# Five, five, three and three partitions for the low side loads, and their zeros written by GpSimd

## The chip, the cores and the metric

The kernel runs on one core of a Trainium2 chip. The metric is the device time of one execution in microseconds. Engines are called PE (TensorE), DVE (VectorE), ACT (ScalarE), POOL (GpSimd) and SP (SyncE, which issues nearly all loads); loads are carried out by 16 transfer engines that the core's queues share.

## The reference

A decode step for 8 sequences of one token each, D = 512. The input x is normalised (layer norm) and goes two ways; all inputs are bf16.

```python
xn = layernorm(x)                                   # [8, 1, 512]
q = xn @ wq                                         # 32 heads of 128
k, v = last 2048 of 8192 rows of k_cache, v_cache   # [8, 8, 2048, 128], each head used by 4 query heads
s = softmax(q k^T / sqrt(128)) v @ wo               # wq [512, 4096], wo [4096, 512]
h = sigmoid(xn @ w_gate) * (xn @ w_up)              # [8, 1792]
g = silu(h @ w_down)                                # w_down [1792, 512]
out = x + s * g
```

The windows of k and v are 67 MB of the 81 MB that are read; w_down has 1792 rows of 1 KB.

## The kernel before, in words

All large tensors are loaded by SP's queue into nine slots of SBUF. A list `todo` holds the loads in a fixed order: w_gate and w_up (two halves each), the main part of w_down, side loads and the two halves of wq mixed, then the tiles of k and v (one of 2 MB for a sequence and half its heads, k three tiles ahead of v), then wo in five pieces that get smaller (12, 8, 6, 4 and 2 of 32 row groups). `pump` takes entries from the list as long as a slot is empty, and `free` gives a slot back and calls `pump` again. A load that reuses a completion semaphore also waits for the earlier load of it; there are eight in turn.

A load into 128 partitions gives each of the 16 transfer engines eight rows. The rows of w_down are divided unevenly: 1280 rows go as ten row groups on 128 partitions (tile `wd_sb`, `want_down`), and the other 512 rows go into the tile `side` by eight small loads (`want_side`). Four of them, the low ones, bring 14 rows of w_down (14336 bytes) into each of `LOW` = 4 partitions, and four, the middle ones, 8 rows (8192 bytes) into each of `MID` = 9 partitions. The low ones lie in partitions 0 to 15, load q taking the partitions q, q + 4 and so on, the middle ones from partition 32 (`M_AT`) on. Partitions 16 to 31 are read by the matmuls of the first eight row groups (68 partitions) and hold zeros, which a DVE memset writes at line 126 before the first side load (partitions 0 to 31, the first eight row groups).

The gated layer's h is computed as [8, 1792] (lines 278 to 301), and two GpSimd copies (lines 309 and 312) put the columns that belong to the side rows in the order of its partitions into `h_side`; its gaps are zeros. PE turns h and h_side (line 320), DVE and ACT copy the result to `hT_sb`, then come the q projection (line 344) and the product with w_down (line 358).

The attention runs over the eight sequences: transposes of k (line 448, copied by DVE at line 453), scores (466), softmax, transposes of the probabilities (556), products with v (577). The last stage is 128 small matmuls with wo (line 699), then two DVE operations and the store of the output.

Of the kernel before, what the change touches and what calls it, by code (L numbers as in the profile page):

```python
# [10 lines left out]
def kernel(  # L11
# [13 lines left out]
    nc = tc.nc  # L25
    P = 128
    B, _, D = A_x.shape
# [59 lines left out]
    def pump():  # L87
        while todo and (empty or not todo[0][0]):
            slot, f = todo.pop(0)
            f(f"slot{empty.pop(0)}") if slot else f()  # L90
# [17 lines left out]

        todo.append((True, f))

    LOW, SF = 4, 14
    MID, SM = 9, 8
    SP = 4 * LOW
    M_AT = 32
    MP = 4 * MID
    MT = 10
    m0 = MT * P
    m1 = m0 + SF * SP
    assert m1 + SM * MP == F
    side = {}  # L120

    def want_side(w, first, at, count, rows, base):
        def f(tag=None):
            if tag:
                t = slots.tile([P, SF, w.shape[1]], bf16, name="side", tag=tag)
                nc.vector.memzero(t[:M_AT, :SM])  # L126
                side["t"] = t
                rows_of[("side", 0)] = (t, tag)
                for r in range(SF):
                    weights[("wd_sb", MT + r)] = t[: M_AT + MP if r < SM else SP, r]  # L130
            last = at + 4 * count
            q0.dma_start(  # L132
                out=side["t"][at + first : last : 4, :rows].rearrange(
                    "p s n -> p (s n)"
                ),
                in_=w[base : base + 4 * count * rows, :].rearrange(
                    "(p s) n -> p (s n)", s=rows
                )[first : 4 * count : 4],
            )

        todo.append((not side, f))
        side["asked"] = True

    def want_down(w):
        def f(tag):
            t = slots.tile([P, MT, w.shape[1]], bf16, name="wd_sb", tag=tag)
            q0.dma_start(
                out=t[:].rearrange("p t n -> p (t n)"),
                in_=w[: MT * P, :].rearrange("(p t) n -> p (t n)", t=MT),
            )  # L150
            rows_of[("wd_sb", 0)] = (t, tag)
            for r in range(MT):
                weights[("wd_sb", r)] = t[:, r, :]

        todo.append((True, f))

    def want_cache(tiles, cache, name, b, i):
# [14 lines left out]
    want_rows("wg_sb", B_w_gate, KT, 0, KT, 2)  # L172
    want_rows("wu_sb", B_w_up, KT, 0, KT, 2)
    want_down(B_w_down)
    sides = [
        (q, *x) for q in range(4) for x in ((0, LOW, SF, m0), (M_AT, MID, SM, m1))
    ]
    for x in sides[:2]:
        want_side(B_w_down, *x)
    for i in range(2):  # L180
        want_rows("wq_sb", A_wq, KT, 2 * i, 2 * i + 2)
        for x in sides[2 + 3 * i : 5 + 3 * i]:
            want_side(B_w_down, *x)
# [7 lines left out]
    for t0, t1 in ((0, 12), (12, 20), (20, 26), (26, 30), (30, RT)):  # L191
# [1 line left out]

    x_bf = work.tile([B, D], bf16, name="x_bf")
    q1.dma_start(out=x_bf[:], in_=A_x.flatten_outer_dims())
    pump()

    ident = consts.tile([P, P], bf16, name="ident")
    make_identity(nc, ident[:])
    ident_f = consts.tile([P, P], f32, name="ident_f")  # L200
    make_identity(nc, ident_f[:])

    perm = consts.tile([P, P], bf16, name="perm")
    nc.vector.tensor_copy(
        out=perm[:].rearrange("k (l p) -> k l p", l=G),
        in_=ident[:].rearrange("k (p l) -> k l p", l=G),
# [13 lines left out]
        out=rstd[:], in_=mv[:, 1:2], func=AF.Sqrt, bias=eps_t[:], scale=1.0  # L220
# [4 lines left out]
        out=xn_bf[:],  # L225
# [8 lines left out]
    for kt in range(KT):  # L234
        nc.tensor.transpose(
            out=xnT_ps[:, kt, :],
            in_=xn_bf[:].rearrange("b (p kt) -> b kt p", kt=KT)[:, kt, :],
# [18 lines left out]
    h_side = work.tile([B, SF, M_AT + MP], bf16, name="h_side")  # L256
# [6 lines left out]
    with nc.allow_low_precision(reason="zeros and a one"):  # L263
        nc.vector.reduce_sum(
            out=band[:], in_=ident[:].rearrange("k (q t) -> k q t", t=RT), axis=AX.X
        )
        nc.vector.reduce_sum(
            out=pick[:], in_=ident[:].rearrange("k (q t) -> k t q", t=RT), axis=AX.X
# [21 lines left out]
    h_bf = ktpool.tile([P, CU * P], bf16, name="h_bf", tag="kT")  # L290
    for k in range(F // FC):
        u_ps = ps_t.tile([B, FC], f32, name="u_ps", tag="t")
        for kt in range(KT):
# [8 lines left out]
            out=h_bf[:B, k * FC : (k + 1) * FC],  # L302
# [3 lines left out]
        )  # L306
    free(rows_of[("wu_sb", 0)])
    hT_ps = ps_m.tile([P, MT + SF, B], bf16, name="hT_ps", tag="m")
    nc.gpsimd.tensor_copy(
        out=h_side[:, :, :SP], in_=h_bf[:B, m0:m1].rearrange("b (p t) -> b t p", t=SF)  # L310
    )
    nc.gpsimd.tensor_copy(
        out=h_side[:, :SM, M_AT:],
        in_=h_bf[:B, m1:F].rearrange("b (p t) -> b t p", t=SM),
    )
    cuts = [h_bf[:B, :m0].rearrange("b (p t) -> b t p", t=MT)[:, t] for t in range(MT)]
    rows = [P] * MT + [M_AT + MP] * SM + [SP] * (SF - SM)
    cuts += [h_side[:, t, : rows[MT + t]] for t in range(SF)]
    for t, x in enumerate(cuts):
        nc.tensor.transpose(  # L320
            out=hT_ps[: rows[t], t, :], in_=x, identity=ident[:B, :B]
        )
    nc.vector.tensor_copy(out=hT_sb[:, :MT, :B], in_=hT_ps[:, :MT])
    for k, t0, t1 in ((M_AT + MP, MT, MT + SM), (SP, MT + SM, MT + SF)):
        nc.scalar.copy(out=hT_sb[:k, t0:t1, :B], in_=hT_ps[:k, t0:t1])
# [41 lines left out]
    for e in range(2):  # L367
# [3 lines left out]
        for r in range(rep):  # L371
            nc.tensor.transpose(  # L372
                out=qT_ps[:, r].rearrange("p g z -> p (g z)"),
                in_=q_bf[:, r * Dh : (r + 1) * Dh],
# [3 lines left out]
            out=qm_sb[:, :, G * e : G * (e + 1), M0 : M0 + rep].rearrange(  # L378
                "p b g r -> p r g b"
            ),  # L380
            in_=qT_ps[:, :, :, :B],
# [14 lines left out]
    for j in range(NB):  # L396
# [15 lines left out]
        out=turn_rows[:].rearrange("k (x l r) -> k x l r", x=NU, l=G),  # L412
        in_=ident[:].rearrange("k (l x r) -> k x l r", x=NU, l=G),
    )
    sel_e = consts.tile([P, 2, Hq], f32, name="sel_e")
    for e in range(2):
        nc.vector.reduce_sum(
            out=sel_e[:, e, :].rearrange("k (i h) -> k i h", i=NQ),
            in_=ident_f[:].rearrange(
                "k (i m e h) -> k e i h m", i=NQ, m=NJ // 2, e=2  # L420
            )[:, e],
# [243 lines left out]
    last = B - 1  # L665
# [47 lines left out]
    for j in range(NB):  # L713
        (q0, q1)[j % 2].dma_start(
            out=out.flatten_outer_dims()[:, j * P : (j + 1) * P],
            in_=y_bf[Z * j : Z * j + B, :],
# [31 lines left out]
```

## Time and profile before

| | us |
|---|---|
| median of 3 runs | 200.63 (200.6 to 200.64) |
| the profiled execution | 200.46 |
| its span, first to last instruction | 198.69 |
| PE busy | 159.2 (80%) |
| DVE busy | 126.7 (64%) |
| ACT busy | 40.5 (20%) |
| POOL busy | 5.7 (3%) |
| mean rate of the loads | 409 GB/s, 81.32 MB |

The profile's first part gives each engine's busy time, its second 40 equal slices of the span, the third the queues with the time of their packets as a share of all 16 transfer engines, the fourth the chain of work that ended last. The timeline and the chain in order of time give start and length in us from the span's start. In the slices the transfer engines are at 9 tenths or more in all but the first and the last two.

### The profile page before, as it was taken

How to read it: one execution, taken by the hardware profiler on the slowest of the kernel's cores; microseconds unless marked ns; L12 is line 12 of the kernel's file. 1: busy time of each engine (PE TensorE's matmuls, PEld its weight loads, DVE VectorE, ACT ScalarE, POOL GpSimd, SP SyncE). 2: the span in 40 equal slices, each digit the busy share in tenths (PEclk: the TensorE clock that was granted, in tenths of full speed). 3: DMA queues.
4: the chain of work that ended last, by engine and by line, in shares of the span. 5: the costliest groups of instructions: out<-in, count | busy, mean ns of one | idle time of the engine just before them, and what ended most of it. 6: DMA issues, size and time to landing. Idle time of an engine off the chain costs nothing.

```text
span 198.7 us, 4852 instructions
## 1 busy us (share of the span) xinstructions
PE 159.2 (80%) x2136; PEld 105.1 (53%) x2136; DVE 126.7 (64%) x259; ACT 40.5 (20%) x95; POOL 5.7 (3%) x15
## 2 busy tenths in 40 slices
PE   0695369998786998799979995999999768976752
PEld 0233125776663565556646654666777456655541
DVE  6824006999795696579667963379789657935201
ACT  3330022006206000700160016000340060071000
POOL 8002000000000000000000000000000000000000
PEclk9999559999999999999999998599999999999975
DMA  6999999999999999999999999999999999999970
GB/s 221 427 442 430 421 429 432 422 429 427 426 435 429 432 426 429 429 429 432 429 426 430 435 424 429 432 426 429 432 426 426 435 422 435 429 434 411 423 287 5
DMA packets 6540, 81.32 MB, mean 409 GB/s; under 512 B 828, under 2 KB 836, under 8 KB 1732
## 3 DMA queue, kind: packets, MB, share of 16 engines
q1 hardware_dynamic: 6472, 81.01, 96.0%
q8 instruction: 16, 0.26, 0.5%
q14 instruction: 4, 0.03, 0.0%
q10 hardware_dynamic: 48, 0.01, 0.0%
HBM read 81.01 MB, written 0.01 MB: 408 GB/s over the span
## 4 chain that ended last, share of the span: by engine, by line
DMA 69%; PE 23%; DVE 6%; issue 1%; SPq 0%
DMA v_sb<-in_A_v_cache_dram 33%; DMA k_sb<-in_A_k_cache_dram 18%; PE kT_ps L448 12%; DMA wo_sb<-in_A_wo_dram 10%; DMA wq_sb<-in_A_wq_dram 8%; PE o_ps L577 4%; PE s_ps L466 3%; DVE kT_sb L453 2%; PE m_ps L607 1%; PE pT_ps L556 1%; DVE side L126 1%; DVE pT_sb L561 1%; PE fin_ps L699 1%; SPq L132 0%; DVE stats L213 0%
## 5 line engine op out<-in xcount | busy, mean ns | idle before, releaser
L453 DVE COPY kT_sb<-kT_ps 128x1024 bf16<-128x1024 bf16 x128 | 83.8, 683 | 29.3 <-PE kT_ps L448 24.8
L448 PE MATMUL kT_ps<-perm,k_sb 128*128 128x128 bf16 x1024 | 73.9, 222 | 3.9 <-DMA k_sb<-in_A_k_cache_dram 3.7
L448 PEld LDWEIGHTS <-k_sb 128*128 128x128 bf16 x1024 | 60.0, 99 | 24.9 <-issue 16.8
L577 PE MATMUL o_ps<-v_sb,pT_sb 128*32 128x256 bf16 (+1 forms) x384 | 34.8, 315 | 9.8 <-DMA v_sb<-in_A_v_cache_dram 8.3
L466 PE MATMUL s_ps<-kT_sb,qm_sb 128*32 128x512 bf16 x256 | 26.0, 396 | 1.4 <-DVE kT_sb L453 1.1
L486 ACT ACTIVATE p_buf<-s_ps,st 32x512 bf16<-32x512 f32 x32 | 21.7, 679 | 15.7 <-DVE st L479 15.4
L577 PEld LDWEIGHTS <-pT_sb 128*32 128x32 bf16 (+1 forms) x384 | 12.8, 100 | 21.7 <-issue 18.8
L597 ACT ACTIVATE o_sb<-o_ps,fac 128x512 f32<-128x512 f32 (+1 forms) x8 | 4.6, 581 | 59.9 <-PE o_ps L577 59.9
L561 DVE COPY pT_sb<-pT_ps 128x1024 bf16<-128x1024 bf16 x16 | 10.8, 676 | 1.8 <-PE pT_ps L556 1.8
L466 PEld LDWEIGHTS <-qm_sb 128*32 128x32 bf16 x256 | 7.1, 93 | 8.3 <-issue 1.7
L556 PE MATMUL pT_ps<-turn_rows,p_buf 128*128 128x128 bf16 x128 | 10.7, 227 | 0.0
L556 PEld LDWEIGHTS <-p_buf 128*128 128x128 bf16 x128 | 9.4, 149 | 0.2 <-issue 0.2
L513 ACT ACTIVATE w_row<-w 1x128 f32<-1x128 f32 x8 | 2.5, 308 | 32.6 <-DVE w L506 32.6
L377 DVE COPY qm_sb<-qT_ps 128x128 bf16<-128x128 bf16 x2 | 1.4, 884 | 11.9 <-PE qT_ps L372 11.9
L344 PE MATMUL q_ps<-wq_sb,xnT_sb 128*32 128x512 bf16 x32 | 3.7, 617 | 5.4 <-DMA wq_sb<-in_A_wq_dram 5.4
L278 PE MATMUL g_ps<-wg_sb,xnT_sb 128*8 128x448 bf16 x16 | 6.3, 575 | 1.1 <-DMA wg_sb<-in_B_w_gate_dram 0.8
L699 PE MATMUL fin_ps<-wo_sb,oP_sb 128*32 128x128 bf16 x128 | 3.8, 274 | 2.7 <-DMA wo_sb<-in_A_wo_dram 2.3
L486 ACT ACTIVATION_READ_ACCUMULATOR p_buf<-s_ps,st 32x1 f32 x32 | 5.9, 184 | 0.0
L479 DVE TENSOR_REDUCE st<-s_ps 128x1 f32<-128x512 f32 x8 | 5.5, 683 | 0.5 <-PE s_ps L466 0.5
L301 DVE TENSOR_TENSOR h_bf<-sig,u_ps 8x448 bf16<-8x448 f32 x4 | 2.4, 608 | 4.1 <-PE u_ps L294 3.7
L344 PEld LDWEIGHTS <-xnT_sb 128*32 128x32 bf16 x32 | 1.2, 125 | 7.1 <-issue 7.1
L607 PE MATMUL m_ps<-ident_f,o_sb 128*128 128x32 f32 x32 | 5.0, 304 | 0.0
(88 smaller groups left out, 84.9 us busy)
## 6 DMA issues: line engine op xcount, KB each, us to landing
k_sb<-in_A_k_cache_dram SPq DMA_DIRECT2D x16, 2048.0 KB
v_sb<-in_A_v_cache_dram SPq DMA_DIRECT2D x16, 2048.0 KB, 30.5
wq_sb<-in_A_wq_dram SPq DMA_DIRECT2D x2, 2048.0 KB, 14.3
wg_sb<-in_B_w_gate_dram SPq DMA_DIRECT2D x2, 896.0 KB
wu_sb<-in_B_w_up_dram SPq DMA_DIRECT2D x2, 896.0 KB, 10.0
wo_sb<-in_A_wo_dram SPq DMA_DIRECT2D x1, 1536.0 KB
wd_sb<-in_B_w_down_dram SPq DMA_DIRECT2D x1, 1280.0 KB
wo_sb<-in_A_wo_dram SPq DMA_DIRECT2D x1, 1024.0 KB
```

Source lines behind the costliest of these rows:

```text
L278: nc.tensor.matmul(g_ps[:], lhsT=xnT_sb[:, kt, :B], rhs=weights[("wg_sb", kt)][:, k * FC : (k + 1) * FC], start=(kt == 0), stop=(kt == KT ...
L344: nc.tensor.matmul(q_ps[e][Z * g : Z * (g + 1), :], lhsT=xnT_sb[:, kt, :], rhs=weights[("wq_sb", kt)][:, c0 : c0 + D], start=(kt == 0), st ...
L448: nc.tensor.transpose(out=kT_ps[:, c, :], in_=k_sb[:, j * CU + h * CH + c, :], identity=perm[:],)
L453: nc.vector.tensor_copy(out=kT[(b, u)][:, h * CH : (h + 1) * CH, :], in_=kT_ps[:])
L466: nc.tensor.matmul(s_ps[b][NR * l : NR * (l + 1), :], lhsT=qm_sb[:, b, i * G + l, o : o + Z], rhs=t[:, :, PG * l : PG * (l + 1)], start=(u ...
L479: nc.vector.tensor_reduce(out=st[b][:], in_=s_ps[b][:], axis=AX.X, op=ALU.max, negate=True)
L486: nc.scalar.activation(out=p_buf[b % 2][rows, :, l, :], in_=s[rows, :].rearrange("k (c p) -> k p c", p=PG), func=AF.Exp, bias=st[b][rows, ...
L556: nc.tensor.transpose(out=pT_ps[:, c, :], in_=p_buf[b % 2][:, :, :, h * CH + c].rearrange("k p l -> k (p l)"), identity=turn_rows[:],)
L561: nc.vector.tensor_copy(out=pT[b][:, h * CH : (h + 1) * CH, :], in_=pT_ps[:])
L577: nc.tensor.matmul(o_ps[r] if b < WIDE else o_ps[r, 0:2], lhsT=pT[b][:, c, r], rhs=x, start=(c == 0), stop=(c == CU - 1), tile_position=(0 ...
L607: nc.tensor.matmul(oT_ps, lhsT=o[:, e, :], rhs=sel[:, e], start=(e == 0), stop=(e == n - 1),)
L699: nc.tensor.matmul(fin_ps[Z * j : Z * (j + 1), :], lhsT=oP_sb[:, t, :], rhs=weights[("wo_sb", t)][:, j * P : (j + 1) * P], start=(t == 0), ...
```

## The change

The four low loads take 5, 5, 3 and 3 partitions in place of 4 each; the total of 16 rows of 14 stays. Load q still takes the partitions q, q + 4 and so on, so the low part now reaches to partition 19 (`SP` = 20), and loads 0 and 1 share one run of w_down's rows, loads 2 and 3 another. Partitions 14, 15, 18 and 19 get no row, so zeros are needed there in all 14 row groups: the memset now covers partitions 0 to 31 with all row groups, 3584 words of 4 bytes each, and is GpSimd's. The call of `pump` that starts the loads stands behind the two `make_identity`, so that this memset is queued behind GpSimd's work for them. The first GpSimd copy of `h_side` becomes two, and the short row groups have 20 partitions in place of 16.

```diff
-    LOW, SF = 4, 14
+    LOW, SF = (5, 5, 3, 3), 14
     MID, SM = 9, 8
-    SP = 4 * LOW
+    SP = 4 * max(LOW)
...
-    m1 = m0 + SF * SP
+    m1 = m0 + SF * sum(LOW)
...
-    def want_side(w, first, at, count, rows, base):
+    def want_side(w, q, at, count, rows, base, of):
         def f(tag=None):
             if tag:
                 t = slots.tile([P, SF, w.shape[1]], bf16, name="side", tag=tag)
-                nc.vector.memzero(t[:M_AT, :SM])
+                nc.gpsimd.memzero(t[:M_AT])
...
-            last = at + 4 * count
             q0.dma_start(
-                out=side["t"][at + first : last : 4, :rows].rearrange(
+                out=side["t"][at + q : at + q + 4 * (count - 1) + 1 : 4, :rows].rearrange(
                     "p s n -> p (s n)"
                 ),
-                in_=w[base : base + 4 * count * rows, :].rearrange(
-                    "(p s) n -> p (s n)", s=rows
-                )[first : 4 * count : 4],
+                in_=w[base : base + of * count * rows, :].rearrange(
+                    "(p q s) n -> q p (s n)", q=of, s=rows
+                )[q % of],
             )
...
-    sides = [
-        (q, *x) for q in range(4) for x in ((0, LOW, SF, m0), (M_AT, MID, SM, m1))
-    ]
+    sides = []
+    for q in range(4):
+        sides.append((q, 0, LOW[q], SF, m0 + q // 2 * 2 * LOW[0] * SF, 2))
+        sides.append((q, M_AT, MID, SM, m1, 4))
...
-    pump()
 
     ident = consts.tile([P, P], bf16, name="ident")
     make_identity(nc, ident[:])
     ident_f = consts.tile([P, P], f32, name="ident_f")
     make_identity(nc, ident_f[:])
+    pump()
...
-    nc.gpsimd.tensor_copy(
-        out=h_side[:, :, :SP], in_=h_bf[:B, m0:m1].rearrange("b (p t) -> b t p", t=SF)
-    )
+    for h in range(2):
+        c = LOW[2 * h]
+        at = m0 + h * 2 * LOW[0] * SF
+        nc.gpsimd.tensor_copy(
+            out=h_side[:, :, : 4 * c].rearrange("b t (e q) -> b t e q", q=4)[
+                :, :, :, 2 * h : 2 * h + 2
+            ],
+            in_=h_bf[:B, at : at + 2 * c * SF].rearrange(
+                "b (e q t) -> b t e q", q=2, t=SF
+            ),
+        )
```

## The prediction

> **What bounds the kernel now.** I read the page's chain of work that ended last, then the queues, then the end of the chain in order of time, and last the single DMA packets that the trace records.
>
> The chain, by engine:
>
> ```profile
> DMA 69%; PE 23%; DVE 6%; issue 1%; SPq 0%
> ```
>
> Two thirds of the last chain is waiting for transfers. The queue rows say how full the transfer engines are:
>
> ```profile
> q1 hardware_dynamic: 6472, 81.01, 96.0%
> q8 instruction: 16, 0.26, 0.5%
> q14 instruction: 4, 0.03, 0.0%
> ```
>
> All loads are on q1, and their packets fill 96% of the span on the mean of 16 engines. What ends the kernel is the chain's tail (start, length, what):
>
> ```profile
> 174.91 19.21 DMA wo_sb<-in_A_wo_dram
> 194.12 0.04 issue
> 194.16 0.62 PE fin_ps L699 x15
> 194.78 0.02 issue
> 194.80 0.43 PE fin_ps L699 x8
> ```
>
> TensorE waits for the last pieces of wo, and the eight matmuls at 194.80 need the very last load. A load is complete when the slowest of its engines is done, so I followed the engines one by one. The packet records have no engine number, but on an engine one packet follows the other within a few ns (a 16384-byte packet every 607 ns), and every load ends with one 4-byte record for each engine it used. A 128-partition load leaves 16 of them, a nine-row side load nine, a four-row side load four. So 16 sequences can be chained, and the side packets (14336 bytes for the low rows, 8192 for the middle ones) show that the same four engines take all low rows and that these four are also among the nine. That makes three kinds of engine. End of the last wo packet, us in the span, a star for each instruction fetch (q8, 16 KB) and a plus for each of the 8 KB fetches of q14 that fell between an engine's packets:
>
> ```
> four engines with low and middle rows   192.73  192.77  193.38+  194.46++
> five engines with middle rows only      190.49  191.09  191.22+  193.26**  193.43**
> seven engines without side rows         189.54  192.08** 192.24** 192.28** 192.88** 193.04** 193.17**
> ```
>
> After the first loads the only time lost is these fetches (0.84 us for each of the two on the last engine, about 1.4 for each q8 one) and 0.5 and 1.1 us near 24 us on two of the seven. The last engine ends at 194.46, the next at 193.43: one engine alone holds the kernel for 1.03 us. Its last landing plus 0.34 is the 194.80 at which the last matmuls start.
>
> **The change part by part.** The profiled execution took 200.46 us, its span 198.69 and 1.77 around it; the median of the runs is 200.63, 0.17 more. I work in the span and take the difference to the median.
>
> *Rows moved.* Of the four low loads two get five rows and two get three. By the nesting seen above, the first three engines keep four rows each, the fourth goes from four to two, and a fifth gets two that had none. A row is one packet of 14336 bytes: its record is 535 ns, the next packet of the engine follows 531 later, and the 4-byte record takes 6, so 537 ns a row and 1.07 us for two. [...]
>
> If the late engine is the fourth, it ends at 194.46 - 1.07 = 193.39, and the last is then the 193.43 of an engine that I take to be untouched. The gain is 194.46 - 193.43 = 1.03 us. It goes through to the end if TensorE is ready: after 189.14 it has 128 small matmuls, the third last batch would be done by 191.06, the next waits for a landing at 191.53 + 0.34 and takes 0.83, the one before the last lands by 192.78 + 0.34 and needs 0.62 to 193.74, and the last eight start at 193.43 + 0.34 = 193.77. That is just enough; a loss of 0.1 is possible.
>
> *The zeros and the wait.* The call that starts the loads moves behind the identities, but SyncE's list of loads keeps its order. The VectorE memset of 1.76 us goes. A GpSimd one of 32 x 3584 words comes in behind the two identities, and SyncE's first side load now waits for it:
>
> ```profile
> 1.52 1.70 POOL masks.py:199 TENSOR_SCALAR_AFFINE_SELECT ident_f<-ident_f 128x128 f32<-128x128 f32 x1
> 3.17 0.69 POOL L253 MEMSET hT_sb<- 128x384 uint32 x1
> 3.79 0.52 POOL L255 MEMSET oP_sb<- 128x512 uint32 x1
> ```
>
> The step from oP_sb to the next start is 0.47 us for 512 words, 0.92 ns each; hT_sb's 0.62 for 384 is 1.6 each. So 3584 words take 3.3 to 5.8 us; I take 3.3, the longer tile being nearer. The select before it took 1.70 beside the VectorE memset where its bf16 twin took 0.29, so the start is 1.8 to 3.2 and the end 5.1 to 9.0. What waits behind it on SyncE:
>
> ```profile
> 2.78 0.66 SPq L147 DMA_DIRECT2D wd_sb<-in_B_w_down_dram  x1
> 3.48 1.64 SPq L132 DMA_DIRECT2D side<-in_B_w_down_dram  x2
> 5.16 0.46 SPq L101 DMA_DIRECT2D wq_sb<-in_A_wq_dram  x1
> 5.70 4.88 SPq L132 DMA_DIRECT2D side<-in_B_w_down_dram  x3
> 12.16 0.34 SPq L101 DMA_DIRECT2D wq_sb<-in_A_wq_dram  x1
> ```
>
> Two side loads, the first half of wq, three side loads. The engines finish wd between 13.93 and 14.86; until then they are fed. The first half of wq was issued 1.68 after the side load and the first packet of the kernel came 1.05 after its issue (0.74 to 1.79), so the memset may end as late as 13.93 - 2.73 = 11.2 before an engine runs dry. At 5.1 to 9.0 the cost is nothing. SyncE has caught up before the wq load at 12.16 or shortly after, and what follows that is not needed by the engines until wq's first half is done, at 18.9.
>
> GpSimd's three memsets (1.5 us in all) move back to end at 6.7 to 10.6; pick_f, at 10.69, is the first that could notice. VectorE, one memset shorter, can have the normalised x about 0.5 us earlier, which buys nothing because TensorE then waits for w_gate until 7.85. It could also be later. [...] Either way TensorE's front work has this cover:
>
> ```profile
> 20.25 1.84 PE L344 MATMUL q_ps<-wq_sb,xnT_sb 128*32 128x512 bf16 x16 [1.02 <-DMA wq_sb<-in_A_wq_dram]
> 26.50 1.90 PE L344 MATMUL q_ps<-wq_sb,xnT_sb 128*32 128x512 bf16 x16 [4.41 <-DMA wq_sb<-in_A_wq_dram]
> ```
>
> Up to 1.02 us of delay disappears before 20.25, up to 4.41 more before 26.50, while three k loads stand in the queues.
>
> *Copies and shapes.* The GpSimd copy of h_side (0.56 us, 8x224) becomes two of the same total; one fixed cost more, between 0 and another 0.56. It delays transposes that sit before the 1.02 us wait. Twenty partitions instead of sixteen in the six short tiles cost no time: the instructions have the same length along the free side.
>
> Sum: -1.03 + 0 + 0 + 0 = -1.03 us, from 200.63 to **199.60**.
>
> **The rivals.**
>
> *The late engine is another of the four (no change).* Then it still has four low rows and ends at 194.46: 200.63. The trace does not number the four. What I can see is whose fetches hold it up: between its two fetches (at 48.0 and 118.7) VectorE ran 125 instructions, and 8 KB at PE's rate of 4272 instructions to 16 fetches of 16 KB is 134, so it serves VectorE's instruction stream. The fetch at 104.6 on another of the four fits ScalarE's 63rd instruction, the one at 177.1, on an engine of the five, SyncE's 82nd. If such streams lie on neighbouring engines, the one across the border is the fifth, and VectorE's is the fourth or one further down. The late engine is also the last of the four to start, its first packet at 2.37 against 1.79 to 1.83, as one served after the others would. Blind the fourth has one chance in four; with both hints I choose 0.68. [...] Under this rival I also count that the fifth engine is one with PE fetches: 193.26 or 193.43 plus 1.07 is 194.33 or 194.50, a gain of 0.13 or a loss of 0.04. Together 0.22.
>
> *The bound is a slow transfer engine elsewhere (no change).* [...] Here 16384 bytes take 611 ns in all 16 sequences wherever no fetch falls, and the three latest engines lie in the first two kinds; I give it 0.02, inside the 0.22.
>
> *The queue runs dry (slower).* If GpSimd is held by VectorE's three memsets after 6.41 (1.66 + 0.91 + 0.91), the memset ends at 9.0 + 3.5 = 12.5 and the engines idle 1.3 us from 13.93. All 16 lose it: 201.9 without the gain above, 200.9 with it. It decides from an end of 11.2 on. Against it: both ends of the cost must be at their worst. 0.10.
>
> **How the numbers follow.** The fourth engine is the late one, with 0.68: 199.6, own range 199.4 to 199.9. No change 0.22, slower 0.10. This kernel's runs differ by 0.02%, and 0.2% (0.4 us) is about what a comparison can tell from nothing; the gain of 1.03 is 0.5%. The range must reach the no-change case, so 199.4 to 200.8; what is left out is most of the slower case.
>
> **What would show it.** In the packets after: low side loads with five, five, three and three 14336-byte packets; the sequence with the two 8 KB fetches holding two of them and ending near 193.4; the last wo matmuls at about 193.8. GpSimd's memset of side should end before 11.2 and SyncE's second wq load be issued near 12.2. If the sequence with two 8 KB fetches still holds four low packets, the identification failed; if there is a gap in all sequences after wd, the wait did.

## The result and the profile after

The changed kernel takes 199.76 us (five runs, 199.69 to 199.85) against 200.63 (five runs, 200.40 to 200.64): a ratio of 0.9959, interval 0.9945 to 0.9974, a gain of 0.87 us. Its profiled execution took 199.72 with a span of 197.9. The prediction was 199.6.

The chain that ended last, by engine, and its tail in order of time (start, length, what), of the changed kernel:

```profile
DMA 67%; PE 26%; DVE 4%; SPq 1%; issue 0%
```

```profile
174.40 18.90 DMA wo_sb<-in_A_wo_dram
193.30 0.04 issue
193.35 0.62 PE fin_ps L707 x13
193.97 0.01 issue
193.98 0.43 PE fin_ps L707 x6
```

The bound is the same, the load of wo, and the last matmuls start at 193.98 where they started at 194.80: 0.82 us, nearly the whole gain, sits in this landing. (The chain names 13 and 6 of the 16 and 8 matmuls; the trace has all of them.) Chained as in the prediction, the packets say which transfer engine is last. End of the last wo packet, us in the span; a star is a 16 KB instruction fetch on that engine (taken to be PE's, whose 4272 instructions are by far the longest stream; from one such fetch to the next it starts 262 of them on the mean), a plus an 8 KB one:

```
four low rows (first three engines)    192.69  192.74  193.38+
two low rows (fourth and fifth)        192.09+  193.29++
middle rows only (four engines)        190.40  191.12  193.57**  193.60**
no side rows (seven engines)           189.83  191.59*  192.43**  192.46**  192.48**  192.72**  192.87**
```

The low loads run on five, five, three and three engines, and the engine with the two 8 KB fetches is one of the two that now hold two low rows, which went there from four or from none. It held four before, so it is the fourth. It ends at 193.29 in place of 194.46. The next engines now set the end, two that hold middle rows only and carry PE's fetches; they ended at 193.26 and 193.43 before.

At the front, the zeros and the loads behind them. GpSimd's memset and VectorE's cast of x in the changed kernel (start, length, engine, line):

```profile
1.52 0.29 POOL masks.py:199 TENSOR_SCALAR_AFFINE_SELECT ident_f<-ident_f 128x128 f32<-128x128 f32 x1
1.75 3.07 POOL L126 MEMSET side<- 32x3584 uint32 x1
```

```profile
2.21 3.25 DVE L211 CAST x_f<-x_bf 8x512 f32<-8x512 bf16 x1 [0.65 <-DMA x_bf<-in_A_x_dram]
```

The same cast in the kernel before:

```profile
3.00 0.49 DVE L211 CAST x_f<-x_bf 8x512 f32<-8x512 bf16 x1
```

SyncE's list and TensorE's rows after the change:

```profile
4.86 1.67 SPq L131 DMA_DIRECT2D side<-in_B_w_down_dram  x2
6.57 0.46 SPq L101 DMA_DIRECT2D wq_sb<-in_A_wq_dram  x1
7.07 3.62 SPq L131 DMA_DIRECT2D side<-in_B_w_down_dram  x3
12.15 0.34 SPq L101 DMA_DIRECT2D wq_sb<-in_A_wq_dram  x1
```

```profile
20.30 1.29 PE L352 MATMUL q_ps<-wq_sb,xnT_sb 128*32 128x512 bf16 x16 [1.84 <-DMA wq_sb<-in_A_wq_dram]
26.56 1.90 PE L352 MATMUL q_ps<-wq_sb,xnT_sb 128*32 128x512 bf16 x16 [4.96 <-DMA wq_sb<-in_A_wq_dram]
```

The side loads start 1.4 us later (4.86, before 3.48), and SyncE has caught up by the second wq load at 12.15 (before 12.16). The cast of x lasts 3.25 us in place of 0.49: it starts inside the memset and ends at 5.46, 0.64 after the memset's end at 4.82. Yet TensorE reaches the q matmuls with 1.84 us to wait (before 1.02), and 4.96 in the second row.

### The profile page after: what moved, and what is told of

It is laid out like the page before. It is cut to its first block, busy times and chain, and to the rows that moved or that the text cites. A ratio compares the mean times of both kernels' runs of the same rounds, so it can differ in the third digit from the quotient of the medians.

```text
span 197.9 us, 4853 instructions
## 1 busy us (share of the span) xinstructions
PE 157.6 (80%) x2136; PEld 104.7 (53%) x2136; DVE 128.4 (65%) x258; ACT 40.5 (20%) x95; POOL 7.5 (4%) x17
## 4 chain that ended last, share of the span: by engine, by line
DMA 67%; PE 26%; DVE 4%; SPq 1%; issue 0%
DMA v_sb<-in_A_v_cache_dram 45%; PE kT_ps L456 12%; DMA wo_sb<-in_A_wo_dram 10%; DMA wq_sb<-in_A_wq_dram 7%; DMA wu_sb<-in_B_w_up_dram 5%; PE o_ps L585 4%; PE s_ps L474 3%; DVE kT_sb L461 3%; PE d_ps L366 2%; PE m_ps L615 1%; PE pT_ps L564 1%; PE q_ps L352 1%; SPq L101 1%; DVE pT_sb L569 1%; PE fin_ps L707 1%; PE qT_ps L380 0%
## 5 line engine op out<-in xcount | busy, mean ns | idle before, releaser
L585 PE MATMUL o_ps<-v_sb,pT_sb 128*32 128x256 bf16 (+1 forms) x384 | 35.9, 326 | 8.5 <-DMA v_sb<-in_A_v_cache_dram 7.0
L585 PEld LDWEIGHTS <-pT_sb 128*32 128x32 bf16 (+1 forms) x384 | 13.4, 104 | 20.6 <-issue 17.4
L352 PE MATMUL q_ps<-wq_sb,xnT_sb 128*32 128x512 bf16 x32 | 3.2, 536 | 6.8 <-DMA wq_sb<-in_A_wq_dram 6.8
L278 PE MATMUL g_ps<-wg_sb,xnT_sb 128*8 128x448 bf16 x16 | 4.5, 452 | 0.3 <-DVE xnT_sb L242 0.3
L707 PE MATMUL fin_ps<-wo_sb,oP_sb 128*32 128x128 bf16 x128 | 3.2, 252 | 1.6 <-DMA wo_sb<-in_A_wo_dram 1.1
```

The source lines that it names most:

```text
L278: nc.tensor.matmul(g_ps[:], lhsT=xnT_sb[:, kt, :B], rhs=weights[("wg_sb", kt)][:, k * FC : (k + 1) * FC], start=(kt == 0), stop=(kt == KT ...
L352: nc.tensor.matmul(q_ps[e][Z * g : Z * (g + 1), :], lhsT=xnT_sb[:, kt, :], rhs=weights[("wq_sb", kt)][:, c0 : c0 + D], start=(kt == 0), st ...
L585: nc.tensor.matmul(o_ps[r] if b < WIDE else o_ps[r, 0:2], lhsT=pT[b][:, c, r], rhs=x, start=(c == 0), stop=(c == CU - 1), tile_position=(0 ...
L707: nc.tensor.matmul(fin_ps[Z * j : Z * (j + 1), :], lhsT=oP_sb[:, t, :], rhs=weights[("wo_sb", t)][:, j * P : (j + 1) * P], start=(t == 0), ...
```

## The experiments

Two theories stood against each other. By the first the gain is the two low rows taken from the one late engine. By the second it comes from the front: VectorE's freed memset and the loads' later start.

**Rows alone.** All zeros by VectorE, the loads started as before:

```diff
-                nc.gpsimd.memzero(t[:M_AT])
+                nc.vector.memzero(t[:M_AT])
...
+    pump()
     ident = consts.tile([P, P], bf16, name="ident")
...
-    pump()
```

> The rows are moved (5, 5, 3, 3), but the zeros stay on VectorE (all 14 row groups, 3584 words) and the loads are started ahead of the identities as before. Theory of the rows: the late engine loses two low rows (1.07 us) and the next ones end it, 199.7 to 199.9. Theory of the front (the gain came from VectorE's freed memset and the later start of the loads): no gain, 200.6; with VectorE's memset about 3.1 us long, by 3584 words at 0.86 ns, the front is even later.

Measured: 199.99 us against 200.68 before in this series, ratio 0.9957 (0.9940 to 0.9973), as for the full change (0.9959). The time lies 0.09 above the expected 199.7 to 199.9, far nearer to it than to the 200.6 of the front. The last engines are again the two with PE's fetches, 193.74 and 193.56, and the fourth ends at 193.26. VectorE's memset ran from 1.54 to 4.58, so the first side load was issued at 4.61, nearly as late as in the changed kernel. This run therefore parts the gain from GpSimd's memset, but not from the later side loads; the next one does that. Two rows of it (GpSimd's select beside VectorE's memset, and the last matmuls):

```profile
1.52 3.30 POOL masks.py:199 TENSOR_SCALAR_AFFINE_SELECT ident_f<-ident_f 128x128 f32<-128x128 f32 x1
```

```profile
194.11 0.43 PE fin_ps L707 x8
```

**Zeros alone.** The changed kernel with four rows in each low load:

```diff
-    LOW, SF = (5, 5, 3, 3), 14
+    LOW, SF = (4, 4, 4, 4), 14
```

> The zeros are GpSimd's and the loads start behind the identities, but the four low loads have four rows each. Theory of the rows: as the kernel before, 200.5 to 200.7, with the late engine at about 194.5 in the span. Theory of the front: as the changed kernel, 199.7 to 199.9.

Measured: 200.48 us, ratio 0.9993 (0.9980 to 1.0005), the time 0.02 below the range of the rows' theory. The engine with the two 8 KB fetches holds four rows and ends at 194.41. The chain's tail, as before the change:

```profile
194.12 0.62 PE fin_ps L707 x16
194.74 0.01 issue
194.75 0.43 PE fin_ps L707 x8
```

So the gain is the rows'; the zeros' move is worth nothing that these runs can tell.

**Half of the move.** Low loads of 5, 4, 4 and 3 rows, each with a run of w_down's rows and a copy of h_side of its own:

```diff
-    LOW, SF = (5, 5, 3, 3), 14
+    LOW, SF = (5, 4, 4, 3), 14
...
-        sides.append((q, 0, LOW[q], SF, m0 + q // 2 * 2 * LOW[0] * SF, 2))
+        sides.append((q, 0, LOW[q], SF, m0 + sum(LOW[:q]) * SF, 1))
...
+    for q in range(4):
+        at = m0 + sum(LOW[:q]) * SF
+        nc.gpsimd.tensor_copy(
+            out=h_side[:, :, q : q + 4 * (LOW[q] - 1) + 1 : 4],
+            in_=h_bf[:B, at : at + LOW[q] * SF].rearrange("b (e t) -> b t e", t=SF),
+        )
```

> Low loads of 5, 4, 4 and 3 rows: the fourth engine keeps three rows, the fifth gets one. Theory of the rows: half of the relief, the late engine at 194.46 - 0.54 = 193.92 or 193.29 + 0.54 = 193.83, so 200.0 to 200.2. Theory of the front: as the changed kernel, 199.7 to 199.9.

Measured: 200.10 us, ratio 0.9976 (0.9962 to 0.9990), as expected. The interval overlaps that of the full change, so it is the packets that place this kernel between the two: the one engine with three low rows carries both 8 KB fetches and is the last, at 193.99. In the tail the last matmuls start at 194.35, between 193.98 and 194.80:

```profile
193.72 0.62 PE fin_ps L702 x16
194.34 0.01 issue
194.35 0.43 PE fin_ps L702 x7
```

**One engine further.** Low loads of 6, 6, 2 and 2 rows in the changed kernel:

```diff
-    LOW, SF = (5, 5, 3, 3), 14
+    LOW, SF = (6, 6, 2, 2), 14
```

> Low loads of 6, 6, 2 and 2 rows: third and fourth engine have two rows, fifth and sixth two. If the sixth engine is none of the two middle-row engines with TensorE's fetches, it ends near 191.5 to 192.2 and the time is that of the changed kernel, 199.7 to 199.9; if it is one of them, it ends at 193.60 + 1.07 = 194.67 and the time is 200.8. The theory of the front expects 199.7 to 199.9 either way.

Measured: 200.77 us, ratio 1.0002 (0.9991 to 1.0013): the whole gain is lost. Among the engines with two low rows is now one with two PE fetches, and it ends at 194.75 (194.67 expected); the engine with the two 8 KB fetches ends at 193.37. So the sixth engine is one that cannot take rows, and the fifth, with one fetch, was the right place for them. The tail shows the one landing that all wait for:

```profile
175.68 19.41 DMA wo_sb<-in_A_wo_dram
195.12 0.32 PE fin_ps L707 x8
```

**A third fetch.** To see whose fetches hold the fourth engine, 64 tiny VectorE memsets were put into VectorE's idle time from 20 to 28 us (59 ns each), in the changed kernel:

```diff
+    idle_t = work.tile([P, 1], f32, name="idle_t")
+    for _ in range(64):
+        nc.vector.memset(idle_t[:], 0.0)
     def fold(out_ps, src, start, stop):
```

> The changed kernel with 64 tiny VectorE memsets in its idle time before 31 us, so that VectorE's stream passes its 320th instruction before the end. Theory of the fetches: a third 8 KB fetch falls on the engine that has two, 0.84 us more there, 193.29 + 0.84 = 194.13 against 193.60, so 200.2 to 200.4; the two old fetches come earlier. Rival (the two fetches are not VectorE's, or lie elsewhere): 199.6 to 199.9, still two on that engine.

Measured: 200.07 us, ratio 0.9970 (0.9959 to 0.9982). Neither time was met: it lies 0.13 below the theory's range and 0.17 above the rival's. The packets decide for the theory. The engine now has three 8 KB fetches, at 26.7, 83.5 and 156.0 (in the changed kernel two, at 49.2 and 118.1), each 0.84 us, and ends last at 194.06, 0.40 after the next. Counted in VectorE's stream, they come when it has started 80, 192 and 320 instructions; in the changed kernel after 69 and 193. So the fetches go with VectorE's instructions.

The profile's chain does not name a load at the end of this kernel:

```profile
190.86 3.52 PE fin_ps L711 x120
194.38 0.02 issue
194.40 0.32 PE fin_ps L711 x8
```

TensorE came to wo later here (190.86, in the changed kernel 190.07), at a granted clock of 0.50 from 192 to 194 us, and the modelled ends of its matmuls fill the time to 194.38. Their starts show that the last eight waited all the same: the 120th matmul started at 194.07, the landing released the next at 194.36, 0.30 after the engine's end as in the kernel before, and it started at 194.40. At the two earlier pieces that had already landed the step from one piece to the next was 0.09 us. The third fetch thus set the end of this execution. What it costs in time is less sure: the medians differ by 0.31 us (200.07 against 199.76) over two series, and the intervals of the two ratios overlap.

**Who held the cast.** In the changed kernel, x cast by ScalarE:

```diff
-    nc.vector.tensor_copy(out=x_f[:], in_=x_bf[:])
+    nc.scalar.copy(out=x_f[:], in_=x_bf[:])
```

> The cast of x is ScalarE's in place of VectorE's, which costs ScalarE one more table load of 1.28 us. If VectorE's cast was held by GpSimd's memset (3.25 us long, where it took 0.49 before), ScalarE's takes about 0.5 us and ends near 3.2, and TensorE's first matmul with w_gate starts near 6.0 to 6.5 in place of 8.09; if the x load or something else held it, the start stays near 8. The time is that of the changed kernel in both cases, 199.5 to 200.1.

Measured, in a single run: 199.60 us. ScalarE's cast ran beside GpSimd's memset and took 0.62 us:

```profile
2.73 0.62 ACT L211 CAST x_f<-x_bf 8x512 f32<-8x512 bf16 x1
```

TensorE's first matmuls with w_gate began at 6.54 in place of 8.09:

```profile
6.54 0.91 PE L278 MATMUL g_ps<-wg_sb,xnT_sb 128*8 128x448 bf16 x2 [0.27 <-DVE xnT_sb L242]
```

It was the memset that held VectorE's cast, and the 1.55 us won buy nothing that one run can show.

**How late the wait may get.** The prediction's slower rival was a queue run dry if GpSimd's memset ended after 11.2. Four kernels repeat that memset:

```diff
-                nc.gpsimd.memzero(t[:M_AT])
+                for _ in range(3):
+                    nc.gpsimd.memzero(t[:M_AT])
```

(twice, and twice behind a shorter one of 8 row groups, three times, four times). Three and four were run first; the two shorter ones followed when three had cost more than expected.

> GpSimd's memset of side done twice; by the 9.68 us that three took it ends at 8.2 in place of 4.8. Theory of the dry queue: no cost, 199.6 to 200.1, and no hole in the transfers. Rival (lateness of the side loads costs in proportion, as zero_3's 2.4 us for 6.6 us could be read): 1.2 us more, 200.9.

> Two memsets of side and a shorter one of 8 of its 14 row groups ahead of them: it ends at about 10.1, 1.3 us earlier than zero_3's and 1.1 ahead of the 11.2. Theory of the dry queue alone: no cost, 199.6 to 200.1. If zero_3's second hole (25 to 27.5 us) has a cause of its own in the late loads behind the wait, it may be left without the first one: 200.2 to 201. Proportional rival: 1.9 us more, 201.7.

> The changed kernel with GpSimd's memset of side done three times, one after the other: it ends at about 1.75 + 3 x 3.1 = 11.0, just ahead of the 11.2 from which the prediction has the queue run dry. Theory of the dry queue: no cost, 199.6 to 200.1. Rival (any lateness of the side loads or of the normalised x goes to the end): 6 us more wait, up to 205.

> The same with four memsets, end at about 14.1, past 11.2. Theory of the dry queue: the first half of wq has its first packet at 14.1 + 1.7 + 1.05 = 16.9 while the engines finish wd at 14.0 to 14.7, so 2.3 to 2.9 us are lost on all engines: 202.0 to 202.7, and a hole in the queue's rate after 14. Rival: the same cost as zero_3, whichever that is, or four thirds of it.

| end of the memsets, us | time, us | ratio to before, interval |
|---|---|---|
| 4.8 (the changed kernel) | 199.76 | 0.9959, 0.9945 to 0.9974 |
| 8.1 (two) | 199.70 | 0.9949, 0.9933 to 0.9966 |
| 10.1 (two and a part) | 199.88 | 0.9958, 0.9943 to 0.9973 |
| 11.4 (three) | 202.15 | 1.0068, 1.0043 to 1.0094 |
| 14.6 (four) | 203.36 | 1.0134, 1.0119 to 1.0149 |

More than 5 us of lateness cost nothing that these runs can tell, then it costs at once; no proportional reading fits. Nor is a late x the cause: VectorE's copy of the turned x starts at 8.79 with two, three and four memsets alike. The expectation of no cost for three memsets missed, because each took 3.2 us in place of 3.1 and the end lay 0.2 past the mark. The windows show the holes (stretch, length, each engine's busy time and its instructions, PE clock, share of the transfer engines, GB/s). Three memsets:

```profile
13.00:15.00 2.00, 2.00 (x11) 0.91 (x10) 0.53 (x3) 1.07 (x2) 0.21 (x1) 1.00 0.97 345
15.00:17.00 2.00, 2.00 (x12) 0.87 (x10) 1.60 (x3) 0.00 (x0) 0.00 (x0) 1.00 0.93 356
17.00:20.00 3.00, 1.51 (x26) 1.14 (x24) 0.83 (x2) 0.00 (x0) 1.55 (x4) 1.00 0.95 385
...
24.00:28.00 4.00, 0.29 (x4) 0.00 (x0) 0.00 (x0) 0.00 (x0) 0.00 (x0) 0.50 0.85 337
```

and the changed kernel:

```profile
13.00:15.00 2.00, 2.00 (x12) 0.93 (x11) 1.27 (x3) 0.14 (x1) 0.00 (x0) 1.00 1.09 463
15.00:17.00 2.00, 1.33 (x14) 0.74 (x11) 1.16 (x2) 0.00 (x0) 0.55 (x2) 1.00 0.99 426
17.00:20.00 3.00, 0.65 (x14) 0.62 (x15) 0.20 (x1) 0.29 (x2) 1.00 (x3) 1.00 1.00 428
...
24.00:28.00 4.00, 1.44 (x16) 0.67 (x19) 0.00 (x0) 0.00 (x0) 0.00 (x0) 0.50 1.02 433
```

Between 13 and 20 us 2 x 118 + 2 x 70 + 3 x 43 = 505 GB/s times us are missing, 1.2 us at 430 GB/s, though the memsets were only 0.2 us too late. From 13 to 15 the rate falls by a quarter (463 to 345) and the share of the engines by a tenth (1.09 to 0.97), so more than half of this is not idle time but packets that take longer. Between 24 and 28 another 4 x 96 = 384 are missing, 0.9 us. Together that is the 2.1 us by which the span grew (200.0 against 197.9). The second hole, in which 11 to 13 of the 16 engines were at work from 25 to 27.5, has no place in the theory, and the kernel with four memsets has none there (438 GB/s). The first load of k had been issued at 22.37; on four engines that stood idle from about 25.0 its packets began only at 27.4. What makes it is left open.

Four memsets show the plain case: 36 GB/s from 15 to 17 us, and 203.36 us, 3.6 over the changed kernel where 2.3 to 2.9 were expected. The first packets after the hole are slow: the first 16384-byte ones take 0.83 to 1.49 us on fourteen of the engines in place of 0.61, which the estimate had left out.

## Why the prediction was right

**What bounds the kernel.** Right. One engine of 16 set the end, and the ends of the engines, chained from the packets, gave the time of every kernel here that moves rows: the last engine at 194.46 (before), 193.60 (the change), 193.99 (half) and 194.75 (one further) goes with 200.46, 199.72, 200.11 and 200.76 in the profiled executions, 6.00 to 6.12 more each time.

**Rows moved.** Right in mechanism. Two rows took 194.46 to 193.29, 1.17 where 1.07 was worked out; half of the move left 193.99. The size that was off is the next engine: 193.43 was taken as untouched, and it ended at 193.60, so that 0.86 was left of 1.03. The two engines with PE's fetches finished w_gate at 6.96 and 6.99 us in place of 6.57 and 6.81: their start differs from one profiled execution to the next, by as much as that. The measured gain of 0.87 us agrees with this 0.86; the two profiled executions differ by 0.74.

**Which of the four it is.** Here a choice was made with 0.68, and it held. The rows with 5, 4, 4 and 3 settle it: the one engine with three low rows is the one with the two fetches. The third fetch shows that they are VectorE's. But the hints did not prove the place, and one of them was chance: the engine started last of the four before, at 2.37, but in the changed kernel at 1.86, with the three others between 1.83 and 1.87. So the right choice was in part luck. The other hint, that the engine with the one fetch at 177 is the fifth, agrees with the rows: in the changed kernel that fetch (176.8) falls on the other engine with two low rows. That the fetch is SyncE's was not tried.

**The zeros and the wait.** Right: no cost. The memset took 3.07 us (3.3 taken), ended at 4.8 (5.1 the lower bound), and every end up to 10.1 was free; 11.4 was not. The 1.70 us select of before had VectorE's 1.76 us memset in the way: it took 0.29 without one, and 3.30 beside the 3.04 us memset of the kernel with the rows alone; both times it ended 0.24 after the memset.

**Copies and shapes.** Right: the two GpSimd copies took 0.69 us together where the one took 0.56. The transposes of 20 partitions took 162 ns each like those of 16, and at a granted clock of 0.50 a product with 20 rows of w_down took 612 ns beside 633 for one with 68.

**The cast of x.** The prediction left open that the normalised x could be later, and it was: the cast started 0.46 us after GpSimd's memset, ended 0.64 after the memset's end and lasted 3.25 us for 0.49. The delay stayed behind TensorE's cover: TensorE still waited 1.84 us for wq. The run with ScalarE's cast shows the same from the other side, 0.62 us beside the memset. What makes VectorE wait for GpSimd no run shows.

**The rivals.** The bound did not move to a slow engine elsewhere; 16384 bytes take 611 ns on all of them. The dry queue exists, but its price was too low: 0.2 us past the mark cost 2.4 us in time, with slow first packets and a second hole whose cause is open.

**How many engines a load takes.** As many as it has rows, in every low load here: two, three, four, five and six rows went to as many engines, always nested, as the prediction had taken from the nine and four of before. The trace gives the engines no numbers, so which of the 16 they are is not shown.

## What to carry to other kernels

Here the end was that of the last transfer engine (the last matmuls started 0.34 to 0.38 us after it in the kernels before and after, with half the move and one further), and the queue's mean share of 96% did not show it: where a stream of loads bounds a kernel, chain the packets of each engine, and see what holds the last one. Small loads that use few engines were a way to even them out, in units of a row (two rows took 1.17 us off the last engine); before moving rows, look at what the receiving engine carries already, instruction fetches included (with 6, 6, 2 and 2 rows one with two PE fetches became the last, at 194.75). A wait put on the issuing engine was free here as long as the queues behind it were full (a memset end of up to 10.1 us), and dear from the moment they were not (2.4 us at 11.4).

## What the runs showed that was not expected

Instruction fetches are part of the balance: an 8 KB fetch cost its engine 0.84 us on the fourth (0.55 to 0.58 on two others), a 16 KB one 1.41, and each engine that carried PE's had two of these in the kernel before, so 2.8 us of 193. Sixty-four idle VectorE memsets put a third fetch on the last engine. After a queue had run dry the first packets took up to 1.5 us in place of 0.61. And a GpSimd instruction that began beside VectorE's memset ended only 0.24 us after it, with VectorE's zeros of all 14 row groups: 3.30 us for a select of 0.29.
